# Linear attention and an FFN in one kernel: all statements, banks and buffers in another order, and half of the output matmuls cut in two

## The chip, the cores and the metric

One core of a Trainium2 chip runs the whole program. The metric is the device time in microseconds (us); lower is better. A core has a matmul engine (TensorE, PE in the profile, with PEld for its weight loads), three elementwise engines (VectorE = DVE, ScalarE = ACT, GpSimd = POOL), and a queue (SyncE = SP) that issues all DMA here. PE accumulates into eight PSUM banks.

## What is computed

A decayed linear attention over 4 batches, 8 heads, 768 tokens and head dimension 64, then a gated FFN on the 3072 x 512 result:

```python
for t in range(S):
    state = gamma * state + einsum('bhd,bhe->bhde', k[:, :, t], v[:, :, t])
    y[:, :, t] = scale * einsum('bhd,bhde->bhe', q[:, :, t], state)
x = y.transpose(0, 2, 1, 3).reshape(3072, 512)
h = ((x @ w1) * (x @ w2)) @ w3          # 512 x 1024, 512 x 1024, 1024 x 1024
out = h @ w_out                          # 1024 x 512
```

## The kernel before

The tokens are taken in 12 steps of 256 (4 batches, three steps each). For a step n the q, k and v of all heads are loaded as f32 (L111; k and v from step 3 on in two halves, L116) and cast to f16 (`cast`, L63 through a helper). q and k are turned so that the head dimension lies on partitions: on PE for steps 0 to 4 (`turn`, `turned`), by a DMA transpose for steps 5 to 11 (`dma_turn`, L359). v is scaled by a decay table on POOL or DVE (`v<-st,VN`). Attention follows in blocks of 128 tokens: `scores` (L403, L412) and `mask` (L429), `kv`/`kvp` (L459), `state` (carried from step to step within a batch), `inter` (L528, what the state gives) with a small copy on ACT as a `fence` (L539) between it and `av` (L554), and `x_out` (L570, L575), which writes the step's x in f16.

The FFN uses that w3 and w_out have nothing between them: at the start w3 is cast and turned (L271, L282), multiplied with w_out (`w3_mm`, L302), and kept as eight f16 tiles W3O (`w3_out`). So a step needs two products of 512 x 1024 and one of 1024 x 512. Steps 0 and 1 do the first two directly (`rows`, L642). From step 2 on they are done with seven block products in place of eight (`prod`, L804): block sums of the weights (`combine`) and of x (`sums`: sodd, seven, spair) are made beforehand, and the products are put together with copies from PSUM (`keep_part`, ACT or DVE; `seed`, L811), an add on DVE (`c12`), an add on POOL or DVE (`c22`) and a final multiply on DVE (`half_h`), which is the gate. Steps 4 and 5, 6 and 7, 8 and 9, 10 and 11 share their products: one matmul has 256 columns, 128 of each step.

The output product of a step has eight matmuls of 128 x 512 for each of its two halves of tokens: `o_part(n, tb, x)` issues four of them (L677) into one bank, and two of its calls make a bank full; `o_copy` (L696, ACT) takes the bank to SBUF; a DMA on SP stores it. The output of steps 0 and 1 and the very last half go through `o_unit` (L665), all eight matmuls at once, the last in column pieces.

Nothing is scheduled by a planner. The kernel is a list of some 900 statements (L893 to L1782), and the order of the list is the order in each engine's queue. Each engine works in order: an instruction that waits holds up all that are behind it on that engine, DMA issues on SP included. Tables of numbers (SLOTS, L73) say which buffer each new tile takes, and arguments of the statements name the PSUM bank (F0 to F2, S0, S1, X0, X1, K).

Of the kernel before, what the change touches and what calls it, by code (L numbers as in the profile page):

```python
# [21 lines left out]
def kernel(  # L22
# [45 lines left out]
    def bank(tag, shape, dtype=FP):  # L68
# [9 lines left out]
        ),  # L78
# [85 lines left out]
    def numbers():  # L164

        nc.gpsimd.iota(key_i[:, :, :], pattern=[[1, 2], [0, H]], base=1 - 128, channel_multiplier=2)
        nc.gpsimd.iota(
            col_i[:, :, :].rearrange("p g (t j) -> p g t j", t=2), pattern=[[128, 2], [1, 2], [2, 64]],
            base=1 - 128, channel_multiplier=0,
        )  # L170
        for h in range(H):
            p = h // 2
            c = place(p, h % 2) * 64
            nc.gpsimd.memset(LGH[:, h : h + 1], -math.log(gam[h]))
            nc.gpsimd.memset(LGP[c : c + 64, p : p + 1], math.log(gam[h]))

    def keeps():
        nc.gpsimd.memset(keep[:, :, :], 1.0)
# [8 lines left out]
    def late_numbers():  # L187
# [7 lines left out]
        nc.gpsimd.memset(keep64[:, :], 1.0)  # L195
# [93 lines left out]
    W3_BANK = {0: "S1", 1: "F1", 2: "X0", 3: "X1", 4: "S0", 5: "K", 6: "S1", 7: "F0"}  # L289
# [324 lines left out]
    def b_unit(n, u, tag):  # L614
# [5 lines left out]
        ("a", 0, 0): ("X0", "F2"),  # L620
        ("a", 0, 1): ("F1", "S0"),
        ("a", 1, 0): ("F0", "S0"),
        ("a", 1, 1): ("F2", "X1"),
        ("b", 0, 0): ("K", "X0"),
        ("b", 0, 1): ("S1", "F1"),
        ("b", 1, 0): ("S1", "S0"),
        ("b", 1, 1): ("F1", "F2"),
# [42 lines left out]

    def o_part(n, tb, x, tag):
        if (n, tb, 0, 512) not in o_ps:
            assert x == 0
            o_ps[n, tb, 0, 512] = bank(tag, [128, 512])
        ps = o_ps[n, tb, 0, 512]
        for f in range(4 * x, 4 * x + 4):
            nc.tensor.matmul(  # L677
                ps[:, :], lhsT=HT[n][:, tb, f, :], rhs=W3O[f][:, :], start=(f == 0), stop=(f == 7),
            )
# [213 lines left out]
    fetch("r2")  # L893
    fetch("r1")
    fetch("r6")
    fetch("r4")
    fetch("r5")
    fetch("wo3")
    fetch("wo1")
    fetch("wo0")  # L900
    fetch("wo2")
    fetch("r3")
    fetch("r7")
    fetch("k0")
    fetch("q0")
    fetch("v0")
    fetch("r0")
    fetch("q1")
    fetch("k1")
    fetch("w12")  # L910
    step_decays()
    identity()
    late_numbers()
    numbers()
    cast_wo(1, "g")
    cast_wo(2, "g")
    cast_w3(3, "g")
    keeps()
    cast_w3(6, "s")
    cast_w3(2, "v")  # L920
    cast_w3_half(1, 0, "v")
    cast_w3_half(1, 1, "v")
    arguments()
    cast_w3_half(4, 1, "v")
    cast_w3_half(4, 0, "s")
    warm(3, "F1")
    warm(8, "X1")
    warm(4, "X1")
    turn_w3(6, "X0")
    warm(3, "X1")  # L930
    turn_w3_half(4, 1, "S0")
    turned_w3_half(4, 1, "s")
    cast_w3(5, "v")
    turned_w3(6, "v")
    warm(2, "X1")
    turn_w3_half(4, 0, "S0")
    turn_w3(2, "S1")
    turn_w3_half(1, 1, "F0")
    turn_w3(5, "F2")
    turn_w3_half(1, 0, "F0")  # L940
    turned_w3_half(4, 0, "s")
    turned_w3(2, "s")
    turned_w3_half(1, 1, "s")
    cast_wo(3, "v")
    cast_wo(0, "s")
    tables()
    turned_w3(5, "v")
    turned_w3_half(1, 0, "v")
    late_arguments()
    w3_mm(4, 3)  # L950
    w3_mm(2, 3)
    w3_mm(6, 3)
    w3_mm(2, 1)
    w3_mm(1, 1)
    w3_mm(5, 3)
    w3_mm(1, 0)
    w3_mm(5, 0)
    w3_mm(5, 1)
    w3_mm(4, 0)
    w3_mm(2, 0)  # L960
    w3_mm(6, 0)
    turn_w3(3, "X1")
    w3_mm(4, 2)
    w3_mm(2, 2)
    w3_mm(6, 2)
    w3_mm(5, 2)
    w3_mm(6, 1)
    w3_mm(4, 1)
    turned_w3(3, "s")
    w3_out(2, "v")  # L970
    w3_out(6, "v")
    w3_out(5, "v")
    cast_w3(7, "s")
    cast("q", 0, "v")
    cast("k", 0, "g")
    cast_v(0, "g")
    cast_w3(0, "g")
    w3_mm(1, 3)
    turn("k", 0, "F0")
    w3_mm(3, 2)  # L980
    w3_mm(1, 2)
    turn("q", 0, "S1")
    turn_w3(7, "F2")
    w3_mm(3, 1)
    w3_mm(3, 0)
    w3_mm(3, 3)
    turned_w3(7, "v")
    w3_out(4, "v")
    turned("k", 0, "s")
    w3_out(3, "v")  # L990
    w3_out(1, "s")
    turned("q", 0, "s")
    cast("q", 1, "g")
    scores(0, ("F1", "F2"), 1)
    w3_mm(7, 2)
    scores(0, ("S0", "X0"), 0)
    kv(0, ("X1", "K"))
    w3_mm(7, 1)
    w3_mm(7, 0)
    w3_mm(7, 3)  # L1000
    mask(0, 1, 1)
    mask(0, 0, 1)
    state(0, 1)
    mask(0, 1, 0)
    state(0, 2)
    mask(0, 0, 0)
    cast_wc(W1, "w1", 2, 1, "g")
    cast_wc(W1, "w1", 2, 0, "g")
    state(0, 3)
    turn_w3(0, "S1")  # L1010
    inter(0, 0, ("F2", "X1"))
    turned_w3(0, "v")
    w3_out(7, "s")
    fence(0)
    cast("k", 1, "s")
    fetch("v1")
    fetch("w10")
    fetch("w11")
    fetch("w13")
    fetch("w21")  # L1020
    fetch("w23")
    fetch("w22")
    turn("q", 1, "X0")
    inter(0, 1)
    av(0)
    w3_mm(0, 1)
    turn("k", 1, "F0")
    w3_mm(0, 2)
    w3_mm(0, 3)
    w3_mm(0, 0)  # L1030
    turned("k", 1, "s")
    w3_out(0, "s")
    turned("q", 1, "v")
    x_out(0, 0)
    x_out(0, 1)
    cast_v(1, "v")
    cast_wc(W1, "w1", 0, 0, "g")
    cast_wh(W1, "w1", 1, 0, "g")
    cast_wh(W1, "w1", 3, 0, "g")
    scores(1, ("X0", "F2"), 0)  # L1040
    rows(W1, 0, 1, 2)
    scores(1, ("S1", "K"), 1)
    kv(1, ("F0", "X1"))
    mask(1, 0, 0)
    mask(1, 1, 0)
    state(1, 1)
    state(1, 2)
    mask(1, 1, 1)
    mask(1, 0, 1)
    cast_wc(W1, "w1", 0, 1, "s")  # L1050
    cast_wh(W1, "w1", 1, 1, "s")
    cast_wh(W1, "w1", 3, 1, "s")
    fetch("w20")
    fetch("q2")
    fetch("k3")
    fetch("k2")
    fetch("v3")
    fetch("q3")
    fetch("v2")
# [3 lines left out]
    fetch("q5")  # L1063
    fetch("k5")
    fetch("k6")
    fetch("q6")
    load("v", 6)
    rows(W1, 0, 1, 0)
    rows(W1, 0, 0, 2)
    rows(W1, 0, 1, 1)  # L1070
    inter(1, 0, ("F0", "X1"))
    rows(W1, 0, 0, 0)
    rows(W1, 0, 1, 3)
    rows(W1, 0, 0, 3)
    rows(W1, 0, 0, 1)
    rows_out("a", 0, 1, 0, "v")
    fence(1)
    cast_wh(W2, "w2", 1, 0, "s")
    cast_wh(W2, "w2", 3, 1, "v")
    cast_wh(W2, "w2", 3, 0, "v")  # L1080
    cast_wh(W2, "w2", 1, 1, "g")
    rows(W2, 0, 1, 1)
    inter(1, 1)
    av(1)
    x_out(1, 0)
    x_out(1, 1)
    cast_wc(W2, "w2", 2, 1, "g")
    cast("q", 2, "g")
    state(1, 3)
    cast("k", 2, "g")  # L1090
    cast_wc(W2, "w2", 2, 0, "v")
    combine(1, 1)
    cast_wc(W2, "w2", 0, 0, "v")
    cast_wc(W2, "w2", 0, 1, "v")
    combine(1, 0)
    rows_out("a", 0, 0, 0, "s")
    rows_out("a", 0, 1, 1, "s")
    late_tables()
    rows_out("a", 0, 0, 1, "s")
    rows(W2, 0, 0, 1)  # L1100
    rows(W2, 0, 0, 3)
    rows(W2, 0, 1, 3)
    rows(W2, 0, 1, 2)
    rows(W1, 1, 0, 2)
    rows(W1, 1, 0, 0)
    rows(W1, 1, 0, 3)
    rows(W2, 0, 0, 2)
    rows(W1, 1, 1, 1)
    rows(W1, 1, 0, 1)
    rows(W2, 0, 1, 0)  # L1110
    rows(W2, 0, 0, 0)
    rows(W1, 1, 1, 0)
    rows(W1, 1, 1, 2)
    rows(W1, 1, 1, 3)
    rows_out("b", 0, 1, 0)
    rows_out("b", 0, 1, 1)
    rows_out("b", 0, 0, 1)
    combine(2, 1)
    combine(2, 0)
    rows_out("a", 1, 0, 1, "s")  # L1120
    rows_out("a", 1, 0, 0, "s")
    rows_out("a", 1, 1, 1, "v")
    rows_out("b", 0, 0, 0)
    combine(3, 0)
    rows_out("a", 1, 1, 0, "s")
    cast("k", 3, "s")
    rows(W2, 1, 0, 3)
    rows(W2, 1, 0, 2)
    rows(W2, 1, 0, 1)
    turn("q", 2, "F0")  # L1130
    rows(W2, 1, 1, 1)
    rows(W2, 1, 1, 0)
    rows(W2, 1, 1, 3)
    rows(W2, 1, 0, 0)
    turn("k", 2, "K")
    o_part(0, 1, 0, "X1")
    rows(W2, 1, 1, 2)
    o_part(0, 0, 0, "X0")
    o_part(0, 1, 1, "X1")
    o_part(0, 0, 1, "X0")  # L1140
    combine(4, 0)
    combine(3, 1)
    rows_out("b", 1, 1, 0)
    rows_out("b", 1, 0, 1)
    rows_out("b", 1, 1, 1)
    rows_out("b", 1, 0, 0)
    combine(4, 1)
    cast_v(2, "g")
    cast("q", 3, "s")
    turned("k", 2, "s")  # L1150
    turned("q", 2, "s")
    o_copy(0, 1)
    o_copy(0, 0)
    turn("k", 3, "F2")
    scores(2, ("S1", "F0"), 1)
    scores(2, ("F1", "K"), 0)
    kv(2, ("S0", "X1"))
    turn("q", 3, "X0")
    turned("k", 3, "s")
    mask(2, 0, 1)  # L1160
# [643 lines left out]
```

## Time and profile before

| | us |
|---|---|
| three runs | 182.23, 178.13, 180.47 (median 180.47) |
| the profiled execution | 178.94 |
| its span in the trace | 177.2 |
| PE busy | 166.6 |
| DVE, ACT, POOL busy | 132.7, 94.9, 85.1 |

The profiled execution is 1.53 us below the median of the runs, and its trace covers 177.2 of its 178.94 us. Times below are in the trace's own count from the span's start. In rows of the trace a matmul's length counts from its issue until its results are out, and matmuls overlap, so the rhythm of a stream is read from the starts of the rows, not from their lengths.

### The profile page before, as it was taken

Reading aid. Unit: us, or ns where it says so; the run is one execution under the profiler, and the core shown is the slowest. Engines: PE = TensorE matmul, PEld = TensorE weight load, DVE = VectorE, ACT = ScalarE, POOL = GpSimd, SP = SyncE. Lnnn points to the kernel's source line nnn. Section 1 sums busy time; section 2 is a strip of 40 time slices with the busy share of each in tenths; the row PEclk is TensorE's granted clock in tenths of the full one; section 3 lists DMA queues with packets and bytes.
Section 4 is the critical chain, followed back from the end, with each engine's and each line's share of the span. In section 5 each row is a group of like instructions: output and inputs, shape, how many; then the busy total and the mean of one; then the engine's idle time right before and its main releaser. Section 6 shows DMA issues by size and latency. Waiting matters only on the chain.

```text
span 177.2 us, 6297 instructions
## 1 busy us (share of the span) xinstructions
PE 166.6 (94%) x2716; PEld 125.5 (71%) x2716; DVE 132.7 (75%) x229; ACT 94.9 (54%) x158; POOL 85.1 (48%) x111
## 2 busy tenths in 40 slices
PE   7499999889999999899899999999999999999993
PEld 2178988668967598686586867777778586878642
DVE  0461479879999699888889998998978658492940
ACT  2266454684549683942566618554683363717232
POOL 7406554464509097579277676444497003402200
PEclk9999999999999999999999999999999999999999
DMA  5999999999999989999999999999992030194174
GB/s 201 389 414 383 303 320 346 407 387 206 263 292 195 252 180 225 179 187 208 240 192 194 144 241 195 228 173 205 231 197 76 0 122 6 68 403 183 51 303 178
DMA packets 76155, 39.72 MB, mean 224 GB/s; under 512 B 53088, under 2 KB 71776, under 8 KB 76128
## 3 DMA queue, kind: packets, MB, share of 16 engines
q1 hardware_dynamic: 76128, 39.33, 89.2%
q8 instruction: 21, 0.34, 0.8%
q14 instruction: 6, 0.05, 0.1%
HBM read 29.36 MB, written 6.29 MB: 201 GB/s over the span
## 4 chain that ended last, share of the span: by engine, by line
PE 62%; DMA 21%; POOL 6%; SPq 3%; DVE 3%; issue 2%; ACT 1%; POOLq 0%; ACTq 0%
PE psF L804 17%; DMA st<-in_moe_w_dram 9%; DMA st<-in_q_dram 7%; PE psS L677 7%; PE psX L677 6%; DMA st<-in_v_dram 5%; PE psS L804 5%; PE psX L804 4%; PE psK L804 3%; PE psF L642 3%; PE psF L677 3%; SPq L111 2%; PE psS L642 2%; PE psX L665 2%; PE psK L677 2%
## 5 line engine op out<-in xcount | busy, mean ns | idle before, releaser
L804 PEld LDWEIGHTS <-wt 128*128 128x128 f16 x384 | 32.0, 98 | 5.5 <-issue 0.6
L66 POOL TENSOR_TENSOR u<-u,p 128x512 f32<-128x512 f32 x16 | 20.3, 1272 | 29.9 <-ACT u L63 26.6
L804 PEld LDWEIGHTS <-w 128*128 128x128 f16 x288 | 24.1, 98 | 6.2 <-issue 1.7
L677 PEld LDWEIGHTS <-ht 128*128 128x128 f16 x168 | 16.0, 98 | 15.8
L63 ACT COPY u<-psF 128x512 f32<-128x512 f32 x32 | 18.3, 588 | 13.2 <-PE psF L804 11.8
L66 POOL TENSOR_TENSOR v<-st,VN 128x1024 f16<-128x1024 f32 x9 | 17.6, 1952 | 9.0 <-DMA st<-in_v_dram 8.9
L804 PE MATMUL psF<-spair,wt 128*128 128x256 f16 x128 | 18.2, 273 | 0.1
L66 DVE TENSOR_TENSOR ht<-psF,u 128x512 f16<-128x512 f32 x19 | 12.9, 686 | 2.3 <-PE psF L804 1.5
L642 PEld LDWEIGHTS <-w 128*128 128x128 f16 x128 | 12.1, 98 | 3.5 <-POOL w L63 1.4
L677 PE MATMUL psX<-w3o,ht 128*128 128x512 f16 x56 | 13.6, 379 | 0.0
L677 PE MATMUL psS<-w3o,ht 128*128 128x512 f16 x56 | 13.2, 379 | 0.0
L302 PEld LDWEIGHTS <-w3t 128*128 128x128 f16 x128 | 12.0, 98 | 1.7
L804 PE MATMUL psF<-xt,w 128*128 128x256 f16 (+1 forms) x92 | 11.0, 254 | 1.7 <-DVE xt L575 0.9
L811 ACT COPY psX<-psF 128x512 f32<-128x512 f32 x12 | 6.8, 577 | 9.8 <-PE psF L804 6.2
L63 ACT CAST k<-st 128x1024 f16<-128x1024 f32 x10 | 10.4, 1044 | 1.6 <-DMA st<-in_k_dram 1.5
L66 POOL TENSOR_TENSOR spair<-xt,spair 128x512 f16<-128x512 f16 x7 | 8.3, 1186 | 5.9 <-DVE spair L66 4.7
L804 PE MATMUL psF<-xt,wt 128*128 128x256 f16 (+1 forms) x88 | 10.5, 253 | 0.2 <-ACT u L63 0.2
L642 PE MATMUL psF<-xt,w 128*128 128x256 f16 x56 | 9.4, 273 | 1.3 <-POOL w L63 1.1
L63 ACT CAST q<-st 128x1024 f16<-128x1024 f32 x7 | 7.3, 1047 | 4.8 <-DMA st<-in_q_dram 4.8
L575 DVE TENSOR_TENSOR xt<-psX,YN 128x512 f16<-128x512 f32 x13 | 8.5, 684 | 1.7 <-PE psX L554 1.6
L429 DVE TENSOR_TENSOR am<-psS,keep 128x512 f16<-128x512 f32 x14 | 9.3, 682 | 0.0
L63 POOL CAST w<-st 128x512 f16<-128x512 f32 (+1 forms) x7 | 5.5, 794 | 6.3 <-DMA st<-in_moe_w_dram 6.2
(205 smaller groups left out, 387.4 us busy)
## 6 DMA issues: line engine op xcount, KB each, us to landing
st<-in_moe_w_dram SPq DMA_DIRECT2D x16, 512.0 KB, 7.9
st<-in_q_dram SPq DMA_DIRECT2D x12, 512.0 KB, 6.2
st<-in_k_dram SPq DMA_DIRECT2D x18, 256.0 KB, 6.1
st<-in_v_dram SPq DMA_DIRECT2D x18, 256.0 KB, 5.3
out_dram<-osb SPq DMA_DIRECT2D x9, 512.0 KB, 3.6
st<-in_moe_w_out_dram SPq DMA_DIRECT2D x4, 512.0 KB, 9.7
st<-in_k_dram SPq DMA_DIRECT2D x3, 512.0 KB, 8.5
st<-in_v_dram SPq DMA_DIRECT2D x3, 512.0 KB, 7.0
```

What stands on the lines that cost most here:

```text
L63: {"v": nc.vector.tensor_copy, "g": nc.gpsimd.tensor_copy, "s": nc.scalar.copy}[eng](dst, src)
L66: (nc.vector if eng == "v" else nc.gpsimd).tensor_tensor(dst, a, b, op)
L111: via.dma_start(t[:, :].rearrange("p (h x) -> p h x", x=2 * D), src.rearrange("h (p t) d -> p h (t d)", t=2))
L302: nc.tensor.matmul(acc[f][:, cols], lhsT=w3t[f][:, g * 128 : (g + 1) * 128], rhs=WO[i][:, r, cols], start=(first and (r, c) == (0, 0)), st ...
L429: nc.vector.tensor_tensor(t[:, :, :, :].rearrange("p a s i -> p (a s) i"), ps[:, :, :, :].rearrange("p a s i -> p (a s) i"), keep64[:, :]. ...
L575: nc.vector.tensor_tensor(XT[n][:, :, :, :].rearrange("p t a (s x) -> p (a s) t x", s=2)[:, :, :, g * 32 : (g + 1) * 32], x[:, :, :].rearr ...
L642: nc.tensor.matmul(rows_ps[w, n, uh][j // 2][:, j % 2, :], lhsT=W[d][:, f * 128 : (f + 1) * 128], rhs=XT[n][:, :, d, :], start=(first and ...
L665: nc.tensor.matmul(ps[:, x * w : (x + 1) * w], lhsT=HT[n][:, tb, f, :], rhs=W3O[f][:, c0 + x * w : c0 + (x + 1) * w], start=(f == 0 and x ...
L677: nc.tensor.matmul(ps[:, :], lhsT=HT[n][:, tb, f, :], rhs=W3O[f][:, :], start=(f == 0), stop=(f == 7),)
L804: nc.tensor.matmul(ps[:, j, :], lhsT=lhsT, rhs=rhs, start=(opens and j == 0 and c == 0), stop=(i in (2, 3, 4) and j == nf - 1 and c == 1), ...
L811: nc.scalar.copy(WB[n, u, "C"][:, :, :], WB[n, u, "A"][:, :, :])
```

## The change

The set of statements is the same: same steps, same products by pairs, same arithmetic. New is the order of the whole list, from the first load on, with other banks and other buffers, and with some statements on another engine:

- The loads have another order. Before: r2 r1 r6 r4 r5 wo3 wo1 wo0 wo2 r3 r7 k0 q0 v0 r0 q1 k1 w12, then v1 and the other weights, then q2 k3 k2 v3 q3 v2 q4 k4 v4 q5 k5 k6 q6 v6, the step-5 transpose of q, v5, that of k, q7 and so on (r are rows of w3, wo of w_out, w those of w1 and w2). Now: r1 r6 r4 r7 wo2 r5 wo1 wo3 wo0 r3 r2 q0 k0 v0 k1 r0 q1, v1 and the weights, then q2 v2 k2 k3 q3 v3 q4 k4 v4 v5 k5 k6 q5 q6 v6 k7, and then the four transposes of steps 5 and 6 in a row.
- The casts of q7 and q10 go from POOL to ACT, those of k6 and k10 from ACT to POOL. Two `c22` of step 6 and two of step 10 go from DVE to POOL, one of step 8 from POOL to DVE, the x sums of step 2 from POOL to DVE. Memsets of small tables at the start go from POOL to DVE.
- 19 of the `o_part` calls (a list, HALVES) issue each of their four 512-column matmuls as two of 256 columns into the same bank, with the weights loaded again: 76 more matmuls and weight loads.

SP, around the transposes of step 5. k_1569 and q_1396 are the casts of k5 and q5 in the kernel before, k_1717 and q_1715 in the changed one; q_1567, k_1707 and q_1721, k_1375 are those of step 6. Before:

```order
L111 DMA st<-in_q_dram 128x8x128
L116 DMA st<-in_v_dram 128x8x64 x2
L359 DMA_TRANSPOSE qT<-q_1396 128x8x128
L116 DMA st<-in_v_dram 128x8x64 x2
L359 DMA_TRANSPOSE kT<-k_1569 128x8x128
L111 DMA st<-in_q_dram 128x8x128
L359 DMA_TRANSPOSE qT<-q_1567 128x8x128
L359 DMA_TRANSPOSE kT<-k_1707 128x8x128
```

Now:

```order
L111 DMA st<-in_q_dram 128x8x128 x2
L116 DMA st<-in_v_dram 128x8x64 x2
L116 DMA st<-in_k_dram 128x8x64 x2
L359 DMA_TRANSPOSE kT<-k_1717 128x8x128
L359 DMA_TRANSPOSE qT<-q_1715 128x8x128
L359 DMA_TRANSPOSE qT<-q_1721 128x8x128
L359 DMA_TRANSPOSE kT<-k_1375 128x8x128
```

The first two loads of q here are q6 before, q5 and q6 now. The load of k7 now stands ahead of all four transposes, and both of step 5 wait for k5's cast, since k's comes first; v5 has moved up.

ACT, in the same place (`fence` is that of step 3; psF_1671 and psF_1679 are the first output bank of step 2). Before:

```order
L539 COPY fence<-psX_1550 64x1
L63 CAST q_1567<-st 128x8x2x64
L63 CAST k_1569<-st 128x1024
L696 ACTIVATE osb<-psF_1671 128x512
L63 CAST k_1707<-st 128x1024
```

Now:

```order
L539 COPY fence<-psX_1531 64x1
L63 CAST q_1715<-st 128x8x2x64
L63 CAST k_1717<-st 128x1024
L701 ACTIVATE osb<-psF_1679 128x512
L63 CAST q_1721<-st 128x8x2x64
```

Two casts stand ahead of the output copy in both: those of q6 and k5 before, those of q5 and k5 now.

POOL, at the gate of step 3 (the two u<-u,p rows are its `c22`; q_1955 is the cast of q7). Before:

```order
L66 TENSOR_TENSOR v_1787<-st,VN 128x1024
L66 TENSOR_TENSOR t_1951<-s_1699,GS 128x256
L66 TENSOR_TENSOR v_1953<-st,VN 128x1024
L63 CAST q_1955<-st 128x8x2x64
L66 TENSOR_TENSOR u_1945<-u_1945,p_1778 128x512
L66 TENSOR_TENSOR u_1949<-u_1949,p_1776 128x512
```

Now:

```order
L66 TENSOR_TENSOR v_1859<-st,VN 128x1024
L66 TENSOR_TENSOR t_1861<-s_1712,GS 128x256
L66 TENSOR_TENSOR u_1967<-u_1967,p_1800 128x512
L66 TENSOR_TENSOR u_1971<-u_1971,p_1798 128x512
L66 TENSOR_TENSOR v_2087<-st,VN 128x1024
```

The cast of q7 no longer stands ahead of the two adds, and one v product has moved behind them.

The core of the diff (the order of the statements itself is left out, but for the first places of the loads):

```diff
-            nc.gpsimd.memset(LGH[:, h : h + 1], -math.log(gam[h]))
+            nc.vector.memset(LGH[:, h : h + 1], -math.log(gam[h]))
...
+    HALVES = [(0, 0, 1), (2, 0, 0), (2, 0, 1), (2, 1, 0), (2, 1, 1), (4, 0, 0), (5, 1, 0), (6, 0, 0), (6, 1, 0), (7, 0, 1), (7, 1, 0), (8, 1, 1), (9, 0, 0), (9, 0, 1), (9, 1, 0), (9, 1, 1), (10, 0, 0), (10, 1, 1), (11, 0, 0)]
...
+        w = 256 if (n, tb, x) in HALVES else 512
         for f in range(4 * x, 4 * x + 4):
-            nc.tensor.matmul(
-                ps[:, :], lhsT=HT[n][:, tb, f, :], rhs=W3O[f][:, :], start=(f == 0), stop=(f == 7),
-            )
+            for c in range(0, 512, w):
+                nc.tensor.matmul(
+                    ps[:, c : c + w], lhsT=HT[n][:, tb, f, :], rhs=W3O[f][:, c : c + w],
+                    start=(f == 0 and c == 0), stop=(f == 7 and c + w == 512), skip_group_check=True,
+                )
...
-    fetch("r2")
     fetch("r1")
     fetch("r6")
     fetch("r4")
+    fetch("r7")
+    fetch("wo2")
     fetch("r5")
-    fetch("wo3")
     fetch("wo1")
+    fetch("wo3")
     fetch("wo0")
```

More of the change, by code (lines that the diff above doesn't have):

```diff
@@ L1002 @@
[L1002 to L1015, printed above, removed]
+    turn_w3(0, "F2")
+    inter(0, 0, ("S1", "X0"))
+    turn("k", 1, "X1")
+    w3_out(2, "s")
+    w3_out(3, "s")
+    fence(0)
+    turned_w3(0, "s")
+    turned("k", 1, "v")
+    cast("q", 1, "g")
@@ L1125 @@
     rows_out("a", 1, 1, 0, "s")
[L1126 to L1143 removed]
+    cast_v(2, "g")
+    cast_v(3, "g")
@@ L1144 @@
+    state(1, 3)
+    rows(W2, 1, 0, 1)
+    rows(W2, 1, 0, 3)
+    rows(W2, 1, 0, 0)
+    turn("q", 2, "F0")
+    rows(W2, 1, 0, 2)
+    rows(W2, 1, 1, 1)
+    rows(W2, 1, 1, 3)
+    turn("k", 2, "S1")
+    rows(W2, 1, 1, 2)
+    rows(W2, 1, 1, 0)
+    o_part(0, 0, 0, "K")
+    o_part(0, 0, 1, "K")
+    cast_v(4, "g")
+    turned("k", 2, "s")
+    cast("q", 3, "s")
+    o_copy(0, 0)
+    cast("k", 3, "s")
+    cast("q", 4, "s")
+    turned("q", 2, "v")
     rows_out("b", 1, 0, 1)
     rows_out("b", 1, 1, 1)
+    rows_out("b", 1, 1, 0)
@@ L1146 @@
     rows_out("b", 1, 0, 0)
[L1147 to L1159, printed above, removed]
+    scores(2, ("X0", "F0"), 0)
+    scores(2, ("S1", "F1"), 1)
+    kv(2, ("S0", "F2"))
+    mask(2, 1, 0)
     mask(2, 0, 1)
-    state(2, 1)
+    combine(4, 0)
```

1019 lines of the change are left out of this document (514 added, 505 removed), and 18 rows, old and new, of the table SLOTS.

## The prediction

> **What bounds the kernel now.** I read the first page of the profile, then the windows (busy time of each engine in stretches of the span), then, where PE is not full, the timeline of PE and the chain of waits. The first page says who is busiest (engine, us, share, instructions).
>
> ```profile
> span 177.2 us, 6297 instructions
> PE 166.6 (94%) x2716; PEld 125.5 (71%) x2716; DVE 132.7 (75%) x229; ACT 94.9 (54%) x158; POOL 85.1 (48%) x111
> ```
>
> PE is busy for 166.6 of 177.2 us; the next, DVE, for 132.7. The windows tell where PE's missing 10.6 us lie; the first column behind the stretch is its length, then busy us of PE, PEld, DVE, ACT and POOL, then the granted clock, the DMA share and GB/s.
>
> ```profile
> 30.00:36.00 6.00, 4.90 (x102) 3.75 (x100) 5.21 (x10) 3.37 (x6) 3.34 (x5) 1.00 1.03 406
> 60.00:75.00 15.00, 14.20 (x295) 11.45 (x293) 13.95 (x26) 10.28 (x16) 10.38 (x12) 1.00 1.02 207
> 75.00:90.00 15.00, 13.79 (x375) 10.85 (x373) 13.06 (x25) 7.24 (x13) 10.14 (x8) 1.00 1.16 212
> 90.00:105.00 15.00, 15.00 (x340) 11.84 (x339) 13.85 (x25) 7.97 (x16) 10.43 (x9) 1.00 1.10 181
> 165.00:172.00 7.00, 7.00 (x40) 3.70 (x38) 5.14 (x8) 2.38 (x4) 1.27 (x1) 1.00 0.47 187
> ```
>
> From 90 us on PE is full at clock 1.00 (15.00 of 15.00, and 7.00 of 7.00 at the end of the stretch), so an order can't shorten that half, only spoil it. Between 30 and 90 us PE is short of work for 1.1, 0.8 and 1.2 us in the three stretches shown. The DMA share there is 1.0 or more: loads come as fast as they can, at 207 GB/s in the middle one, which makes 2.5 us for a load of 512 KB (524 KB / 207). The timeline of PE names each stop; in brackets stands the idle time before the row and what ended it.
>
> ```profile
> 36.22 0.39 PE L642 MATMUL psF<-xt,w 128*128 128x256 f16 x2 [1.09 <-POOL w L63]
> 61.72 1.07 PE L804 MATMUL psF<-xt,w 128*128 128x128 f16 x16 [0.19 <-DVE xt L570]
> 69.72 1.90 PE L677 MATMUL psF<-w3o,ht 128*128 128x512 f16 x8
> 71.45 0.61 PE L804 MATMUL psF<-xt,wt 128*128 128x128 f16 x8
> 73.53 0.61 PE L804 MATMUL psF<-xt,w 128*128 128x128 f16 x8 [0.60 <-ACT osb L696]
> 79.67 0.42 PE L412 MATMUL psS<-qT,kT 64*64 64x64 f16 x28
> 81.47 0.61 PE L804 MATMUL psF<-xt,wt 128*128 128x128 f16 x8 [0.23 <-ACT u L63]
> 85.95 1.03 PE L804 MATMUL psF<-xt,w 128*128 128x256 f16 x8 [0.87 <-DVE xt L575]
> ```
>
> The reader is to see two things. Where PE doesn't stop, a row starts before the last one ends (69.72 + 1.90 = 71.62, but the next starts at 71.45): 0.17 us of overlap. A stop loses its idle time and this overlap, so the five stops here cost 1.26, 0.36, 0.77, 0.40 and 1.04 us, 3.8 together. And each has another cause. The chain of waits shows those of the last three (start, us, what).
>
> ```profile
> 63.88 6.96 DMA st<-in_q_dram
> 71.82 1.04 ACT k L63
> 72.88 0.61 ACT osb L696
> 75.21 5.81 DMA st<-in_q_dram
> 81.08 1.04 POOL q L63
> 82.12 2.47 POOL u L66 x2
> 84.61 0.61 DVE ht L66
> 85.22 1.88 DVE xt L575 x3
> 87.72 1.16 POOL spair L66
> 88.93 0.60 PE psF L804 x4
> ```
>
> The load of q6, issued at 63.88, lands at 70.84; ACT casts it, then k5 (until 72.86), and only then copies step 2's output bank out (72.88 to 73.49), for which PE waits. The load of q7 lands at 81.03; POOL casts it for 1.04 and only then does the two adds of step 3's gate (u), DVE the gate (ht) and behind it x of step 4 (xt, three of them), for which PE waits at 85.95.
>
> **The change part by part.** PE's work up to the scores of step 5 is the same number of the same statements in both orders, so what counts is how far each stop is longer or shorter.
>
> *Start.* The products of w3 with w_out begin when the first turned tiles and two w_out tiles are there.
>
> ```profile
> 12.70 0.60 PE L302 MATMUL psS<-wo,w3t 128*128 128x256 f16 x4
> 13.14 0.60 PE L302 MATMUL psX<-wo,w3t 128*128 128x256 f16 x4
> 11.71 0.69 DVE L63 CAST wo<-st 128x1024 f16<-128x1024 f32 x1
> 13.02 1.04 POOL L63 CAST wo<-st 128x1024 f16<-128x1024 f32 x1 [5.92 <-DMA st<-in_moe_w_out_dram]
> ```
>
> Before, POOL's cast starts at 13.02 on the landing of wo1, the seventh load. In the new order wo1 is the seventh load again, is cast on DVE (0.69 by the row above it), and is ready at 13.7; the second product needs it, where the second product of before started at 13.14. With a first product at 12.7 again, +0.6. The bounds: 0, if wo1 lands one load earlier, and +1.1 (POOL's 1.04 in the place of 0.69, and some queueing on DVE). I take +0.6. The memsets now on DVE run while nothing has landed, and cost nothing; if they did, the first DVE casts would be late.
>
> *Weights of w1 and w2.* The stop of 1.26 us at 36.22 waits for a weight load and its cast on POOL. The new order casts four such tiles on ACT in a row and has the fence of step 1 behind them; I find the same tile last, landing in the same eighth place of that group, and enter 0. Bounds: -1.26, if it goes, and +1.4, a cast and a half of 1.04, if the fence behind them becomes the wait.
>
> *The output unit of step 1.* It now stands between x of step 2 and the first product that needs x, so its eight matmuls cover DVE's xt: the stop at 61.72 goes, -0.36. What is late next is PE's own work.
>
> *The bank of step 2's output.* In the new order ACT casts q5 and k5 ahead of the copy, before it was q6 and k5. q5 is now the 13th load counted from q2, as q6 was: it lands at 70.84 again, and the stop of 0.77 stays. 0; bounds -0.77 and +1.
>
> *Transposes of step 5.* SP, and what they take to land (minimum, median and maximum over the seven of q).
>
> ```profile
> 68.97 2.56 SPq L359 DMA_TRANSPOSE qT<-q  x1
> 72.89 1.82 SPq L359 DMA_TRANSPOSE kT<-k  x1
> DMA to landing us min/median/max: 4.9/5.9/6.7
> ```
>
> Before, that of q was out at 68.97 and that of k at 72.89, right behind k5's cast. Now k7 and v6 are issued ahead of both, and k's, with the cast of k5 at the same time, goes at 72.9 and holds SP for 1.8; q's follows at 74.7. It lands between 79.6 and 81.4, by the median at 80.6. PE stands at the scores of step 5 with the same work behind it as before (row at 79.67, first pieces at 79.6), moved by +0.6 - 0.36 to 79.8. So a stop of 0.8 (bounds 0 and 1.6 by those landings). The stop of 0.40 at 81.47, two products later, waits for ACT's copy of u; ACT has that time to catch up now, and it goes: net +0.4. Queued behind the waiting scores on PE is all the rest.
>
> *q7's cast.* With it on ACT, later, POOL's two adds start when their inputs are there and not at 82.12. The 1.04 us stop needs them 0.9 earlier, and has 1.04 more: it goes, -1.04. On ACT that cast stands ahead of the fence of step 5, where ACT is busy for 7.24 of 15 us, and is hidden; without that slack it would cost 1.04.
>
> *x sums of step 4.* The chain shows PE waiting for POOL's spair (87.72 to 88.88). In the new order the third sum stands behind the fourth on POOL, and a product needs it: I enter +0.1, bounds -0.2 and +1.2 (one more spair).
>
> *The halves.* The last rows show both kinds side by side: eight matmuls of 512 columns, then 16 pieces that cover eight times 512 columns.
>
> ```profile
> 170.66 1.73 PE psS L677 x8
> 172.39 1.76 PE psX L665 x16
> L677 PE MATMUL psX<-w3o,ht x56: 379/379/379, 50.5 to 170.3; 128*128 128x512 f16 x56
> L665 PE MATMUL psX<-w3o,ht x32: 246/272/299, 56.2 to 173.9; 128*128 128x256 f16 x16, 128*128 128x320 f16 x8, 128*128 128x192 f16 x8
> ```
>
> 1.76 against 1.73 us: 0.03 for eight splits, so 76 splits cost 76/8 x 0.03 = 0.3 us, all of it on PE's path.
>
> Here a rule of the Trainium skill speaks against the change. "TensorE: Matmul & The Clock Gate", section "Back-to-back issue gap", says that in a stream of weight loads and matmuls the spacing is about 131 ns at 512 columns and 81 ns at 128, and that a formula which gives 216 at 512 is for a lone matmul. By it a 256-column piece would take at least 98 (between its two figures), and 76 splits 76 x (2 x 98 - 131) = 4.9 us, an estimate. The trace does not agree: 1.73 us for eight at 512 columns is 216 ns each in a stream with weight loads.
>
> *From 90 us on.* No gain is possible where PE is full. I walked each engine's queue with the durations of the rows and found no wait longer than its cover; the tightest are the last adds of steps 10 and 11, now four on POOL at 1.24 each (82.12, 2.47 for two), about 1 us ahead of the output product that needs them, and the transposes of step 11, 1.5 us ahead of their scores. I enter 0, with one stop like the largest of before, +1.0, as the upper bound of each.
>
> *End.* The last product, copy and store are the same, and the stores before them are out by then: 0.
>
> Sum: 0.6 + 0 - 0.36 + 0 + 0.4 - 1.04 + 0.1 + 0.3 + 0 = 0.0. On the profiled execution's 178.94 that is 178.9; on the median of the runs, 1.53 higher, 180.5.
>
> **The rivals.**
>
> *The loads come in time everywhere.* If every load that ends a stop now comes earlier by the new order, the stops at 36.22, 61.72, 73.53, 81.47 and 85.95 all go: -3.8 us, and with the halves' +0.3, and nothing lost at the start, 180.5 - 3.5 = 177.0; with the 0.1 of the third sum gone as well and one of the small waits before 36, 176.6. For it: the stops are all waits of this kind. Against it: loads saturate the DMA engines in this stretch, and an order moves a late load, it doesn't remove it.
>
> *Step 5's transposes decide.* Queued behind k7 and v6, they may land as late as the slowest kind of load does:
>
> ```profile
> st<-in_moe_w_out_dram SPq DMA_DIRECT2D x4, 512.0 KB, 9.7
> ```
>
> Issued at 74.7 and landing 9.7 later, at 84.4, q's transpose stops PE for 4.6 us where I entered 0.8: 180.5 + 3.8 = 184.3. It decides, against the 2% bound, from a landing at 84.2. For it: the DMA share of 1.16 there, and three loads in the queue at 2.5 us each. Against it: none of seven transposes took over 6.7 us, in the same crowd.
>
> *The weights' casts on ACT.* The fence of step 1 behind four casts: +1.4, 181.9, within 2%. For it: they stand in one queue. Against: before, three of four stood there too.
>
> *Halves at a full matmul each.* Were PE to pay for each piece what the rows show as its length, 76 x (2 x 0.272 - 0.379) = 12.5 us and 193.0 us. The Trainium skill's spacing, named above, would give its 4.9 and 185.4. Rows 170.66 and 172.39 speak against both.
>
> **How the numbers follow.** The forecast, stops moved and none removed in sum, 178.5 to 183: 0.60. Loads in time, 176.6: 0.08. Transposes late, 184.3: 0.15. Casts on ACT, 181.9: 0.12. Halves dear, 185.4 or more: 0.05. The predicted time is that of the forecast, 180.5. Below lies the rival with the loads, which counts as faster (2% of 180.47 is 3.6 us, about what a measurement of this kernel can tell from no change; its runs alone differ by 4.1): the range starts at 177.5, a third of that case being milder. Above, the range reaches to 184.6, over the transposes' case, and leaves out the dear halves. So faster (below 176.9) has 0.07, slower (above 184.1) 0.17: two thirds of the transposes' case, the halves, and a little from stops after 90 us. The rest, 0.76, is within 2%.
>
> **What would show it right or wrong.** In the new profile PE's first w3 product starts near 12.7 and the second near 13.7; no stop stands before the first product of step 2's second half; one of about 0.6 waits for ACT's osb near 73; the scores of step 5 start near 80.6 behind a DMA into qT; and no stop of 0.9 near 86 waits for xt. Eight split matmuls of an output part take as long as four whole ones. From 90 us to the tail PE is full. Wrong it is if PE has idle time in a stretch after 90 us, or if a whole stop of more than 1.5 us stands anywhere in the front.

## The result and the profile after

Over 20 runs each, the changed kernel took 180.94 us in the median (179.23 to 182.9), the kernel before 178.56 (177.39 to 183.96). Some executions of every kernel come out a per cent or more above its others; the ratios here and below leave them out, and the table of starts leaves out the profiles of the fifth and the eleventh experiment, which fell on such executions. The ratio is 1.0105, 95% interval 1.0070 to 1.0141. So the changed kernel is slower by about 1%, some 1.9 us: clear of noise, and within the 2% that were called no change.

Against the 180.5 us of the forecast it came out at 180.94, but the forecast stood on 180.47, the median of three runs of before, and over 20 runs that median is 178.56. The forecast change was 0.0. The profiled execution of the changed kernel (179.38 us, span 177.7) lies only 0.44 us over that of before; the two profiles show less difference than the runs do.

The first page and four windows of the changed kernel:

```profile
span 177.7 us, 6448 instructions
PE 167.7 (94%) x2792; PEld 132.6 (75%) x2792; DVE 125.1 (70%) x239; ACT 104.0 (59%) x171; POOL 77.8 (44%) x88
...
30.00:36.00 6.00, 6.00 (x152) 4.63 (x149) 5.62 (x12) 4.80 (x8) 3.75 (x5) 1.00 1.03 409
60.00:75.00 15.00, 13.26 (x297) 12.13 (x296) 10.93 (x24) 10.40 (x17) 7.70 (x8) 1.00 1.05 224
75.00:90.00 15.00, 14.76 (x388) 11.70 (x386) 12.74 (x27) 9.62 (x17) 9.18 (x8) 1.00 1.10 195
90.00:105.00 15.00, 14.96 (x340) 11.66 (x339) 13.61 (x24) 9.84 (x18) 9.84 (x8) 1.00 1.30 201
```

PE is full between 30 and 36 us, where before it lacked 1.1; it lacks 1.74 between 60 and 75, where before it lacked 0.8; and it lacks 0.24 between 75 and 90, where before it lacked 1.2. The stops moved. The timeline of PE names them (idle time and what ended it in brackets):

```profile
13.70 0.60 PE L302 MATMUL psS<-wo,w3t 128*128 128x256 f16 x4 [0.21 <-DVE wo L63]
23.55 0.62 PE L367 MATMUL psF<-ident,k 128*128 128x128 f16 x8 [0.27 <-POOL k L63]
36.38 0.61 PE L642 MATMUL psX<-xt,w 128*128 128x256 f16 x4 [0.19 <-ACT w L63]
71.34 1.91 PE L681 MATMUL psF<-w3o,ht 128*128 128x256 f16 x16 [1.74 <-DVE ht L66]
80.36 0.45 PE L412 MATMUL psS<-qT,kT 64*64 64x64 f16 x32
88.84 1.03 PE L809 MATMUL psF<-spair,wt 128*128 128x256 f16 x8 [0.16 <-POOL spair L66]
```

One large stop is left, at 71.34, and it is one that the forecast doesn't have. The chain of waits leads back from it:

```profile
62.25 0.76 SPq L116
63.01 0.05 issue
63.06 5.09 DMA st<-in_k_dram
68.16 0.02 issue
68.18 0.04 POOLq L63
68.22 0.08 issue
68.31 1.04 POOL k L63
69.34 1.23 POOL u L66
70.57 0.02 issue
70.60 0.70 DVE ht L66
71.30 0.04 issue
71.34 1.91 PE psF L681 x16
...
75.65 4.67 DMA qT<-q
80.32 0.04 issue
80.36 0.45 PE psS L412 x32
```

The load of k6 lands at 68.16. Its cast now stands on POOL, ahead of step 2's first gate add (u); the add waits for the cast, DVE's gate (ht) for the add, and PE's first output part of step 2 for the gate. PE stops for 1.9 us (1.74 idle, and the overlap of 0.17). Further on the transpose of step 5's q, out at 75.65, lands at 80.32, and the scores start behind it.

Many statements of PE have the same amount of PE work ahead of them in both orders. Their starts in the two profiles (us), and the difference, tell where time is won and lost. For the scores of step 5, whose pieces are mixed with others of `kv` in some orders, it is the time at which the same number of matmul columns has been issued:

| the statement | before | changed | difference |
|---|---|---|---|
| turn of the last row of w3 | 27.97 | 29.02 | +1.05 |
| first product of step 2's second half | 61.72 | 61.02 | -0.70 |
| first product of step 3 | 73.53 | 73.96 | +0.43 |
| scores of step 5 | 79.64 | 80.36 | +0.72 |
| first product of step 4 and 5 | 85.95 | 85.57 | -0.38 |
| their product that needs spair | 88.93 | 88.84 | -0.09 |
| the state's part of step 9 | 124.67 | 125.14 | +0.47 |
| the last output unit | 172.22 | 172.61 | +0.39 |

One thing in the words on the kernel before is to be set right: only step 1's output and the very last half go through `o_unit`; step 0's goes through `o_part` like the others.

### The profile page after: what moved, and what is told of

It is laid out like the page before. It is cut to its first block, busy times and chain, and to the rows that moved or that the text cites. A ratio compares the mean times of both kernels' runs of the same rounds, so it can differ in the third digit from the quotient of the medians.

```text
span 177.7 us, 6448 instructions
## 1 busy us (share of the span) xinstructions
PE 167.7 (94%) x2792; PEld 132.6 (75%) x2792; DVE 125.1 (70%) x239; ACT 104.0 (59%) x171; POOL 77.8 (44%) x88
## 3 DMA queue, kind: packets, MB, share of 16 engines
q1 hardware_dynamic: 76128, 39.33, 89.5%
## 4 chain that ended last, share of the span: by engine, by line
PE 59%; DMA 24%; SPq 7%; POOL 5%; issue 1%; DVE 1%; ACT 1%; POOLq 0%
PE psF L809 18%; DMA st<-in_moe_w_dram 8%; PE psX L681 7%; DMA st<-in_v_dram 5%; SPq L111 5%; PE psS L681 5%; PE psS L809 5%; DMA st<-in_moe_w_out_dram 4%; PE psF L681 4%; PE psX L809 3%; PE psK L809 3%; DMA st<-in_k_dram 3%; DMA qT<-q 3%; POOL v L66 2%; PE psK L681 2%; PE psF L642 2%
## 5 line engine op out<-in xcount | busy, mean ns | idle before, releaser
L66 POOL TENSOR_TENSOR u<-u,p 128x512 f32<-128x512 f32 x19 | 24.0, 1269 | 32.8 <-ACT u L63 29.2
L681 PEld LDWEIGHTS <-ht 128*128 128x128 f16 x244 | 23.5, 98 | 11.3 <-issue 1.9
L681 PE MATMUL psX<-w3o,ht 128*128 128x256 f16 (+1 forms) x96 | 16.2, 308 | 0.0
L63 ACT CAST q<-st 128x1024 f16<-128x1024 f32 x10 | 10.3, 1044 | 4.5 <-DMA st<-in_q_dram 4.4
L809 PE MATMUL psF<-xt,w 128*128 128x256 f16 (+1 forms) x104 | 12.4, 253 | 0.0
L681 PE MATMUL psF<-w3o,ht 128*128 128x256 f16 (+1 forms) x56 | 9.8, 318 | 1.7 <-DVE ht L66 1.7
L63 POOL CAST k<-st 128x1024 f16<-128x1024 f32 x5 | 5.2, 1037 | 13.8 <-DMA st<-in_k_dram 7.1
L681 PE MATMUL psS<-w3o,ht 128*128 128x256 f16 (+1 forms) x60 | 9.7, 308 | 0.0
L701 ACT ACTIVATE osb<-psX 128x512 f32<-128x512 f32 (+2 forms) x10 | 5.6, 555 | 6.5 <-PE psX L681 5.7
L302 PE MATMUL psS<-wo,w3t 128*128 128x256 f16 x64 | 9.0, 273 | 0.2 <-DVE wo L63 0.2
```

What stands on the lines that cost most here:

```text
L63: {"v": nc.vector.tensor_copy, "g": nc.gpsimd.tensor_copy, "s": nc.scalar.copy}[eng](dst, src)
L66: (nc.vector if eng == "v" else nc.gpsimd).tensor_tensor(dst, a, b, op)
L302: nc.tensor.matmul(acc[f][:, cols], lhsT=w3t[f][:, g * 128 : (g + 1) * 128], rhs=WO[i][:, r, cols], start=(first and (r, c) == (0, 0)), st ...
L681: nc.tensor.matmul(ps[:, c : c + w], lhsT=HT[n][:, tb, f, :], rhs=W3O[f][:, c : c + w], start=(f == 0 and c == 0), stop=(f == 7 and c + w ...
L701: nc.scalar.activation(o_tile(n, tb)[:, c0:c1], o_ps.pop((n, tb, c0, c1))[:, :], AF.Copy, scale=final_scale)
L809: nc.tensor.matmul(ps[:, j, :], lhsT=lhsT, rhs=rhs, start=(opens and j == 0 and c == 0), stop=(i in (2, 3, 4) and j == nf - 1 and c == 1), ...
```

## The experiments

Theory A: each stop is lost to the end, so the cast of k6 on POOL costs what its stop costs. In the first four runs it has two forms: A1, that cast alone costs the time; A2, the transposes of step 5 are a second wait right behind it, and each wait hides the other. Theory B: the loss lies elsewhere. Theory C (it came up with the first four runs): PE's place up to about 95 us is set by what arrives late (the loads, and, as it turned out, PE's own instructions), so a stop that is taken away comes back at the next late arrival. All times are ratios to the kernel before, run beside the experiment on the same chip; e1 to e4 share one set of those runs, e5 to e8 a second, e9 to e12 a third. Starts in the profile of each experiment (one execution each), for the same statements as above:

| run | ratio, 95% interval | step 3 | scores 5 | step 4 | spair | last unit |
|---|---|---|---|---|---|---|
| before | 1 | 73.53 | 79.64 | 85.95 | 88.93 | 172.22 |
| changed | 1.0105 (1.0070 to 1.0141) | 73.96 | 80.36 | 85.57 | 88.84 | 172.61 |
| e1 changed again | 1.0049 (1.0004 to 1.0094) | 75.46 | 81.58 | 86.93 | 90.20 | 173.76 |
| e2 k6 behind | 1.0044 (1.0008 to 1.0081) | 73.81 | 80.47 | 85.68 | 88.96 | 172.60 |
| e3 transposes first | 1.0090 (1.0047 to 1.0133) | 73.72 | 79.83 | 85.18 | 88.46 | 173.20 |
| e4 both | 1.0056 (1.0020 to 1.0092) | 72.19 | 78.31 | 83.68 | 86.95 | 172.47 |
| e5 no halves | 1.0025 (0.9982 to 1.0068) | | | | | |
| e6 before, k6 on POOL | 1.0057 (1.0028 to 1.0087) | 73.19 | 79.33 | 84.90 | 87.98 | 171.25 |
| e7 changed, 512-byte rows | 1.0095 (1.0068 to 1.0122) | 73.33 | 79.44 | 86.18 | 89.44 | 173.60 |
| e8 before, 512-byte rows | 1.0068 (1.0024 to 1.0112) | 72.60 | 78.71 | 86.27 | 90.23 | 174.07 |
| e9 changed, wo1 sixth | 1.0117 (1.0072 to 1.0162) | 74.89 | 81.01 | 86.36 | 89.63 | 174.11 |
| e10 before, q7 on ACT | 1.0002 (0.9959 to 1.0045) | 72.57 | 78.68 | 84.34 | 87.38 | 170.93 |
| e11 before, halves | 1.0111 (1.0057 to 1.0164) | | | | | |
| e12 all mended | 1.0062 (1.0042 to 1.0083) | 73.14 | 79.25 | 84.60 | 87.87 | 172.68 |

**e1: the changed kernel again**, without an edit.

> The changed kernel as it is, once more, for a second profile. Theory A (a load of k6 whose landing decides, cast on POOL ahead of step 2's gate adds): the stop ahead of the first output part of step 2 is there again, 1 to 3 us long, and its length follows the start of the cast of k6 on POOL; time 180.2, 1% over before. Theory B (the stop of 1.9 us in the profile was an accident of that execution, the loss lies elsewhere): the stop is under 0.5 us and another one has its place.

The stop is there again, and longer, as the cast starts later. POOL, and PE in the same profile:

```profile
69.81 1.04 POOL L63 CAST k<-st 128x1024 f16<-128x1024 f32 x1 [6.83 <-DMA st<-in_k_dram]
70.81 1.26 POOL L66 TENSOR_TENSOR u<-u,p 128x512 f32<-128x512 f32 x1
...
72.84 1.91 PE L681 MATMUL psF<-w3o,ht 128*128 128x256 f16 x16 [1.94 <-DVE ht L66]
```

The cast starts 1.50 us later than in the first profile (69.81 against 68.31) and so does the output part (72.84 against 71.34): the landing of k6 sets both. The place is as theory A has it. The time, 0.5% over before, is lower than the first 1%, with overlapping intervals. In this profile the turn of k0 at 24.45 waited 1.00 us for POOL's cast of k0, where the first waited 0.27: these two executions of one kernel differ by about a microsecond at the front alone. So the stop is no accident of one execution, as theory B had it.

**e2: the cast of k6 behind the gate adds.**

```diff
-    cast("k", 6, "g")
...
     c22(2, 1)
+    cast("k", 6, "g")
```

> The cast of k6 stands behind step 2's two gate adds on POOL; nothing else is changed. Theory A1 (that cast alone costs the time): PE's stop at 69.4 goes, about 0.6 of it comes back where ACT's output copy stands behind two casts, the rest, 1.3 us, is gained: 178.9. Theory A2 (the step-5 transposes are the next wait and end where they ended): the scores of step 5 start at 80.3 again, with a stop of about 1.4 ahead of them, and the time is the changed kernel's within 0.3: 180.0. Theory B (the loss lies elsewhere): the time is that of the changed kernel, and there is no stop at the scores of step 5.

PE's timeline:

```profile
39.40 0.21 PE L528 MATMUL psK<-qT,t 64*64 64x128 f16 x1 [1.00 <-ACT fence L539]
73.81 1.05 PE L809 MATMUL psF<-xt,w 128*128 128x128 f16 x16 [0.41 <-ACT osb L701]
80.47 0.45 PE L412 MATMUL psS<-qT,kT 64*64 64x64 f16 x32 [0.34 <-DMA qT<-q]
```

The stop at 71 is gone; the output copy behind ACT's two casts is the next, as theory A2 has it, and the scores of step 5 then wait for the transpose and start at 80.47, where A2 had 80.3. The wait there is 0.34 and not 1.4, because this execution had lost 1.0 at 39.40 to the fence of step 1, which is the forecast's rival of the weights' casts on ACT. The last unit starts at 172.60, the same as without the edit. The time (1.0044) is that of e1 beside it (1.0049): A1's gain of 1.3 us isn't there (the difference is 0.1 us, with about 1.0 to either side). It doesn't tell A2 from B.

**e3: the transposes of step 5 ahead of the load of k7; e4: both edits.**

```diff
     load("v", 6)
+    dma_turn("k", 5)
+    dma_turn("q", 5)
     load("k", 7)
-    dma_turn("k", 5)
-    dma_turn("q", 5)
```

> The two transposes of step 5 are issued ahead of the load of k7, behind v6, in the order k, q; all else as changed. Theory A (PE is late by the stop at 69.4 and reaches the scores of step 5 as their transposes land): they land 1.5 to 3 us earlier and nothing is gained, 0.0 to -0.2. Rival (the transposes of step 5 are what the changed kernel waits for): -1.0 or more.

> Both edits: the cast of k6 behind the gate adds, and the step-5 transposes ahead of the load of k7. Theory A2 (two waits in a row, each hidden by the other): -1.3 us against the changed kernel, 178.9, though each edit alone gives 0.2 or less. Theory A1 (the cast alone): the same as with the cast alone. Theory B (the loss lies elsewhere): 180.2, the changed kernel's time.

e3 alone won nothing (1.0090), as theory A had it; the rival (-1.0) is out. e4 is the telling one in the profiles. PE reaches the spair product of step 4 at 86.95, 1.9 us ahead of the changed kernel, and starts the last unit at 172.47, 0.14 ahead. What took the lead back, in e4's timeline of PE:

```profile
86.95 1.03 PE L809 MATMUL psF<-spair,wt 128*128 128x256 f16 x8 [0.17 <-POOL spair L66]
89.48 0.92 PE L809 MATMUL psF<-spair,wt 128*128 128x256 f16 x7 [0.81 <-issue]
95.04 0.22 PE L528 MATMUL psF<-qT,t 64*64 64x64 f16 x2 [0.81 <-ACT fence L539]
```

and ACT at that place:

```profile
93.27 1.05 ACT L63 CAST k<-st 128x1024 f16<-128x1024 f32 x1 [2.19 <-DMA st<-in_k_dram]
94.22 0.59 ACT L701 ACTIVATE osb<-psS 128x512 f32<-128x512 f32 x1
94.83 0.15 ACT L539 COPY fence<-psF 64x1 f32<-64x1 f32 x1
```

The second stop is a load again: k8 lands near 93.2, its cast stands on ACT ahead of step 6's fence, and PE waits. The first has no releaser ("issue": the engine waited for nothing that the profile shows), and it falls inside one product, behind its first matmul. In time e4 (1.0056) is level with e1 beside it (1.0049), so the 1.3 us that A2 expected to win aren't there. So neither A1 nor A2 as they stood; theory C was made from this. By time alone theory B isn't out: with both waits gone the kernel is as slow as with them.

**e5: the changed kernel without the halves; e11: the kernel before with them.**

```diff
-    HALVES = [(0, 0, 1), (2, 0, 0), ...]
+    HALVES = []
```

In e11 the diff of `o_part` above is put into the kernel before, with the same list.

> The changed kernel with whole 512-column matmuls in all output parts (HALVES empty); all else as changed. By rows 170.66 and 172.39 of before: -0.3 us, inside the interval, and PE's position in the list is gained only behind 95 us. Rival (a piece costs a full spacing of its own, 65 ns more per split): -5 us. Theory C (loads set PE's place up to 95 us): the pieces before that cost nothing, and 0.2 is gained at most.

> The kernel before with the 19 output parts of the changed one cut into 256-column pieces; nothing else changed. By the rows: +0.3 us (0.015 a part of four splits), 178.8. Rival (a split costs a full spacing more): +5 us. Rival (152 more PE instructions are supplied late): one more instruction packet, and a stop without a releaser of 0.5 or more.

Both runs' times say more than the rows do: the kernel before with halves is 1.1% slower (1.0 to 2.9 us, by five runs), and the changed kernel without them is at 1.0025, not clear of before and below its own 1.0105 and 1.0049. (The changed kernel was not run beside e5.) Of the edits made to the kernel before, the halves cost the most time. In the rows a split costs next to nothing. From the changed kernel's timeline of PE, 16 pieces and the product behind them:

```profile
161.72 1.91 PE L681 MATMUL psX<-w3o,ht 128*128 128x256 f16 x16
163.47 0.60 PE L809 MATMUL psK<-spair,w 128*128 128x256 f16 x4
```

163.47 - 161.72 is 1.75 us for the columns of eight whole matmuls, against 1.73 before (172.39 - 170.66): 19 parts at half of 0.02 are 0.2 us. The 5 us rival is out by both. The rival with late instructions is met by half: e11's trace has one instruction packet more (22 for 21, see the last section), but no stop of PE of 0.5 without a releaser. What the rest of the 1 to 2 us in the runs is stays open: no profile here shows it.

**e6: the kernel before with the cast of k6 as the changed one has it.**

```diff
+    cast("k", 6, "g")
     c22(2, 0)
...
-    cast("k", 6, "s")
```

> The kernel before with the cast of k6 taken from ACT and put on POOL ahead of step 2's gate adds, as the changed kernel has it. Both theories expect the stop: the load lands near 69.1, PE's first output part of step 2 starts near 72.1 in place of 69.7. Theory A (a stop is lost to the end): +2.4, less 0.8 that the late output copy no longer costs, +1.6. Theory C (the landing of later loads sets PE's place): the stops at 73.5, 81.5 and 86 shrink by as much, products of step 4 start at 86.0 again, and the time is that of before within 0.3.

The load came earlier in this profile than expected, and the stop is small:

```profile
67.11 1.04 POOL L63 CAST k<-st 128x1024 f16<-128x1024 f32 x1 [0.27 <-PE psX L804]
68.11 2.50 POOL L66 TENSOR_TENSOR u<-u,p 128x512 f32<-128x512 f32 x2
...
70.16 1.89 PE L677 MATMUL psF<-w3o,ht 128*128 128x512 f16 x8 [0.61 <-DVE ht L66]
```

The stops at 73.5 and 86 are gone, and step 4 starts 1.05 us earlier than in the profile of before; 0.24 of that was there before the edit could act (61.48 against 61.72). The runs are 0.6% (0.3 to 0.9) slower all the same. So theory A's 1.6 us is just outside the interval and theory C's 0.3 is missed too. The profiled execution (177.92 us) is the fastest of the twelve, so it isn't a picture of their mean; that k6 lands later in the others, as it does in both profiles of the changed kernel, is likely but not shown.

**e7 and e8: rows of 512 bytes.** The k and v of steps 3 to 11 are loaded as one DMA with 512-byte rows; the numbers then stand in wrong places, so the attention of these steps is left out in effect.

```diff
-        if nm == "q" or n < EO:
+        if True:
```

> The changed kernel, but k and v of steps 3 to 11 are loaded in rows of 512 bytes, one DMA each in place of two of 256-byte rows; the same bytes then stand in other places, so the attention of these steps is left out in effect. Theory C (the loads pace PE between 60 and 95 us): the stops at 71, 80 and 90 go and 2 to 3 us with them, 177.5. Theory A (the order of the casts on POOL and ACT costs the time, whatever the loads): the stop at 71 stays within half a us, 179.8.

> The kernel before with the same loads in rows of 512 bytes. Theory C: the stops at 73.5, 81.5 and 86 go, -2 us, 176.5; with both kernels freed of late loads, what is left between them is the start (+0.7 to +1.1 for the changed one), the halves (+0.3) and the weights' stop (-0.9): 0 to 0.5. Theory A: -0.5 or less, and the changed kernel stays 1.5 over it.

Half of this came as theory C had it. In e7 PE runs through the place of the large stop without one:

```profile
70.25 0.62 PE L809 MATMUL psF<-xt,wt 128*128 128x128 f16 x8
70.71 1.91 PE L681 MATMUL psF<-w3o,ht 128*128 128x256 f16 x16
72.45 1.04 PE L681 MATMUL psX<-w3o,ht 128*128 128x256 f16 x8
```

and the scores of step 5 start 0.9 us earlier in both kernels (79.44 and 78.71). In this profile the order of the casts makes no stop once the load is early: theory A's "the stop stays" is out. But the time was not 2 us less in either kernel (1.0095 and 1.0068). In e8's timeline of PE the lead is lost at once:

```profile
83.72 0.32 PE L554 MATMUL psS<-am,v 64*64 64x64 f16 x17
86.02 0.31 PE L554 MATMUL psS<-am,v 64*64 64x64 f16 x15 [1.98 <-issue]
```

A stop of 2 us inside a group of 32 like matmuls, with no releaser. What it is stands in the last section.

**e9: wo1 sixth in the changed kernel.** r5 is loaded behind wo1; its cast, turn and copy move back, w_out's first cast behind them.

```diff
-    fetch("r5")
     fetch("wo1")
+    fetch("r5")
```

> The changed kernel with wo1 loaded sixth instead of seventh (r5 behind it) and r5's cast, turn and copy moved back to suit. Both theories: the first w3 product starts near 12.3 instead of 12.9, the second follows without a stop, and PE is 0.7 to 0.9 us further on at 16 us. Theory A (a stop is lost to the end): -0.7, 179.5. Theory C (the landing of later loads, and the supply of PE's instructions, set its place up to 95 us): the lead is gone by 72 us, where PE waits for k6's cast again until its landing, and the time is that of the changed kernel within 0.3.

The first product starts at 12.52 and the second at 12.96, so the stop at 13.70 is gone; but the lead behind them is 0.1 us (15.77 against 15.88 for the same product), not 0.7, as the first product came later than expected and the turn of r5 waits now. At 72.28 PE waits for the gate again (1.63 idle), as both theories of the middle have it. 1.0117: no gain, and too small an effect at the start to judge A or C by.

**e10: q7's cast on ACT in the kernel before.**

```diff
-    cast("q", 7, "g")
+    cast("q", 7, "s")
```

> The kernel before with the cast of q7 on ACT instead of POOL, at the same place of the list; nothing else changed. The stop of 1.0 us at 86 goes under every theory. Theory A: -1.0 to the end, 177.4. Theory C: PE gets to the products of step 4 a microsecond sooner and stops there for what the loads or the supply of instructions withhold, most of it back by 97 us: within 0.4 of before.

In the profile the stop at 86 is gone, step 4 starts at 84.34, 1.6 us ahead of before, and the last unit at 170.93, 1.3 ahead. Part of that lead was there before the edit could act (the scores of step 5 start at 78.68, 0.96 ahead). The runs say 1.0002 (0.9959 to 1.0045), where theory A had 0.9945 and theory C 1.0: nearer to C, and A just outside the interval. The median of all its twelve runs is 179.45, against 178.35 of before: no gain either way.

**e12: all edits at once**, with the cast of k8 behind step 6's fence and no halves.

```diff
-    cast("k", 8, "s")
...
     fence(6)
+    cast("k", 8, "s")
```

> All at once on the changed kernel: wo1 sixth, the cast of k6 behind step 2's gate adds, the step-5 transposes ahead of the load of k7, the cast of k8 behind the fence of step 6, whole output parts. Theory A: -0.7 at the start, -1.3 from the middle, -0.8 at 95, -0.2 by whole parts, 177.2, a microsecond under the kernel before. Theory C: stops move again, unnamed ones take their place near 85 to 92 us, and the time is that of the kernel before within 0.5.

PE is 1.35 us ahead of before at the first product of step 4 (84.60), and 0.46 behind at the last unit. New stops stand behind it, with releasers this time, each behind ACT; what made ACT late there was not tested:

```profile
89.82 1.03 PE L809 MATMUL psF<-spair,wt 128*128 128x256 f16 x8 [0.47 <-ACT u L63]
111.72 0.60 PE L809 MATMUL psF<-spair,wt 128*128 128x256 f16 x4 [0.48 <-ACT psF L816]
```

1.0062 (1.0042 to 1.0083): theory A's gain is out; the lead was lost as C has it, and the time is 1.1 us over before, more than C's half a microsecond. No version beat the kernel before.

## Why the prediction was right, and where it was wrong

The time was forecast at 180.5 and is 180.94; the class, no change that 2% can tell, is right. That the two times lie so close is luck: the sum was 0.0, the measured change is +1.9 us in the runs (+0.4 in the profiles), and the base of the forecast, 180.47, was by chance 1.9 us above what 20 runs gave for the kernel before. By the prediction's own last sentence ("a whole stop of more than 1.5 us stands anywhere in the front") its account of the front is wrong: there is one, 1.74 idle at 71.34. By its own steps:

- **Start, +0.6: right.** The second product starts at 13.70, where 13.7 was forecast, released by the DVE cast of wo1. A further 0.4 was lost at 23.55, behind POOL's cast of k0; that stop was not in the sum, and in e1 it was 1.2.
- **Weights, 0: wrong in size.** Of the 1.26 us stop 0.36 is left at 36.38, a gain of 0.9. The rival on the same place, the fence of step 1 behind ACT's casts, is real too: 1.00 idle in e2, 0.64 in e9, none in the first profile. (Its bound of +1.4 was called a cast and a half of 1.04, which is 1.6.)
- **Output unit of step 1, -0.36: right.** No stop is left there.
- **Bank of step 2's output, 0: hidden.** The stop didn't show at all in the changed kernel, since PE came 1.9 us late; with the cast of k6 behind the adds it is there (0.41 idle at 73.81), as forecast.
- **Transposes of step 5: right by landing, wrong in cost.** The scores start at 80.36, by the landing at 80.32; 80.6 was forecast. The cost was 0.3 at most (the difference grows from 0.43 to 0.72 on the way there) instead of 0.8, because PE came late.
- **q7's cast, -1.04: right.** No stop stands at 86. **x sums of step 4, +0.1: right** (0.33 against 0.29). **Halves, +0.3: not settled.** By the rows it is 0.2; by the runs the halves cost 1.0 to 2.9 us in the kernel before (e11), and no profile shows where. If that holds for the changed kernel too, this is the term that was mis-sized.
- **What the sum left out is the step that failed in the front.** "I walked each engine's queue with the durations of the rows and found no wait longer than its cover" was said of the time from 90 us on; ahead of it I priced the places where before had a stop, and not each cast that moved. That of k6 went from ACT to POOL, ahead of the adds of step 2's gate, and made the stop of 1.9 us in the profile. It is the same mechanism as q7's cast ahead of the adds of step 3, which the prediction read off the trace and priced in the other direction. The list of the change names it; no term does.
- **From 90 us on, 0: nearly right.** PE lacks 0.04 of 15 us between 90 and 105, and nothing between 105 and 172; the place in the list slips by 0.5 from the spair product to the last unit, of which the halves explain 0.2 at most.

That the two profiles differ by only 0.4 us although a stop of 1.9 was missing in the sum has a reason: the stop at 71 swallowed the stops behind it that the sum had counted (0.77 at the output bank, most of 0.8 at the transposes). The profiles of e2, e3 and e4 show that swallowing, with one execution each: PE is at the spair product 0.1 us behind and 0.4 ahead of the changed kernel with one edit, and 1.9 ahead with both. But none of these edits brought the time below that of e1, run beside them, so that the stop at 71 is what makes the changed kernel 1% slower is not shown. Of single edits to the kernel before, the halves alone make it as slow (e11, 1.1%), k6's cast half as much slower (e6, 0.6%). Of the 1.9 us in the runs, the profiles show 0.4 to 1.5 at the last unit (172.61 and 173.76 against 172.22); how they are shared between k6's landing, the front's stops and the halves is not settled.

## What to carry to other kernels

Where loads saturate the DMA engines and engines work in order, look at each cast of a freshly loaded tile and ask what is queued behind it: a cast that waits for a landing ahead of work that PE needs turns the landing into PE's stop, on whichever engine it stands. Don't add up stops that lie behind one another, ahead of the same late arrivals: a later one is paid only by a PE that comes early enough, so taking away one of several moved nothing here, nor did taking away two. And with run-to-run differences of a microsecond, one profile of each kernel shows what PE waits for, but not the sign of a change of 1%; nor do three runs of before make a base for it (180.47 against 178.56).

## What the runs showed of the hardware that was not expected

PE's own instructions come by DMA, and can be late. The page of the changed kernel lists them as a queue of their own (packets, MB, share):

```profile
q8 instruction: 22, 0.36, 0.9%
```

Each packet is 16384 bytes; the kernel before has 21. In the changed kernel's trace they start some 4 to 9 us apart up to 117 us. The stops without a releaser follow such packets: in e8 a packet ends at 84.5 and PE goes on at 86.0; in e7 at 84.5 and 85.8; in e4 at 87.9 and 89.5; in e3 at 89.4 and 91.1; in the changed kernel at 88.8 and 90.5, where the stop is only 0.2. That is 1.3 to 1.7 us from packet to PE each time.

And they fall on a grid. Counting PE's records (matmuls, weight loads and 14 of its sequencer's), the stop comes behind 2753 of them in e7 and e8, two kernels of different order, and behind 3009 in e3, e4 and the changed one: 256 apart, which at 16384 bytes a packet is 64 bytes an instruction. Smaller stops elsewhere are on the same grid: behind 1729 at 64.4 us in e1, behind 4033 at 120.0 us in e8. The number of packets goes with the number of groups that begin on this grid (at 193, 449 and so on): 21 groups and 21 packets in the kernels without halves, with 5446 records, 22 and 22 in those with halves, with 5598.

The grid holds where PE does not stop as well. In all 14 traces no group starts less than 1.2 us behind the end of its packet (288 groups), and wherever PE stops ahead of a group it is within 1.7 us of that end. So between 82 and 92 us, where attention issues many small matmuls, the supply of instructions is close to PE's pace: the kernel before passes such a group at 84.75 us with 1.7 us. A PE that gets there earlier can run dry (e8), but need not: e6 and e10 come to that group 0.25 and 0.90 us earlier than before does, without a stop.

Why a packet is late is shown in part. Where the DMA engines are over 80% busy in the 3 us around it, the first record of a group is followed by the packet of the next group after 1.95 us in the median; where they are under 30% busy, that packet starts 0.55 us ahead of it. So packets come later where loads and transposes fill the same DMA engines. No run changed this alone: that these loads are the cause is likely but not shown.
